# Backward attention loop of an adaLN block: the rows of a head side by side in DRAM, and dQ of two chunks in one PSUM bank

## The chip, the core and the metric

One core of a Trainium2 chip. The time is device microseconds for one execution of the whole program (forward and backward of one block), as the median over runs.

## The reference

The function is one transformer block with conditioning, and the program computes its output and the gradients of nine inputs (x, the attention and MLP weights and biases, the condition c and w_mod). Cut to what matters here:

```python
def _A_ref(x, wqkv, wo):                       # B, S, D = 1, 2048, 512; H = 32; Dh = 16
    q, k, v = ...                              # (x @ wqkv), split by heads
    scores = einsum('bhqd,bhkd->bhqk', q, k) * Dh ** (-0.5)
    p = softmax(scores, axis=-1)
    o = einsum('bhqk,bhkd->bhqd', p, v)
    return o.transpose(0, 2, 1, 3).reshape(B, S, D) @ wo

h = layernorm(x) * (1 + ca) + sa
x = x + ga * _A_ref(h, A_wqkv, A_wo)
h = layernorm(x) * (1 + cb) + sb
x = x + gb * _B_ref(h, B_w1, B_b1, B_w2, B_b2)  # MLP with squared ReLU
_out, _vjp = jax.vjp(_f, A_x, A_wqkv, ...); _grads = _vjp(grad_out)
```

The attention's backward part needs, for each head, E = exp(scores) again, dP = dO V', dS = E * (dP - delta), and from these dV = E' dO, dK = dS' Q and dQ = dS K. A head has only 16 channels and 2048 x 2048 scores, so these products have a short side of 16 and everything is about moving [128 x 512] blocks of scores through the engines.

## The kernel before

The program has four parts: the projections, the forward attention with the MLP and its gradients woven in, the last chunk of the MLP, then the backward attention loop, and the final projections of the gradients. The change is in the backward loop and in what feeds it.

**How the loop is tiled.** Heads go in eight groups of four (`HG`, here called a head for short). Partitions 32h to 32h+15 of a tile hold the 16 channels of head h of the group; partition 32h+16 holds an extra row (the score bound m beside q, minus delta beside dO, ones beside k and v), so one matmul with 32 rows gives scores minus bound, or dP minus delta. A unit is 128 queries by 512 keys for the four heads; four units (512 queries) make a chunk; a head has 4 x 4 chunks (`kc` over keys outside, `qc` over queries inside), the loop 128 chunks.

**What a unit does.** `score` (L1603): for each of four heads one matmul into a PSUM bank, taken in turn from three banks A, B, C. `expo` (L1609): ACT takes the exponential into `E_u`. `dp_pair` (L1623, L1625): two matmuls for a pair of heads into one of two double banks `psD_u`, then DVE multiplies with `E_u` into `dS_u` (four buffers of two units each). `k_quad` (L1663) and `v_quad` (L1672): four matmuls each, for the four heads in column groups of PE, summing dK and dV of 512 keys in the bank `accVK`; ACT moves that out after 16 units (L1675).

**dQ.** It needs dS with keys on the partitions. `transpose_unit` issues DMA transposes on SP's queue, two units in one DMA (L1640) or one (L1638). For every second chunk the last of its four units is turned by PE instead (`pe_turn`, L1653) and copied by ACT (L1769). So of two chunks seven units go by DMA (three doubles, one single) and one by PE. `dq_quad` (L1690) multiplies the turned tile `dsT` (three buffers of a chunk) with the K rows of all 2048 keys, kept in SBUF as `KS_tok`, and sums a chunk in the bank C. Of each group of 32 rows of that bank only 16 hold dQ; the other 16 come from the neighbour's columns and are not used. `dq_out` moves the bank out with ACT (L1700 for the first key block, else L1703), and POOL adds it to `dQacc` (L1708).

**What sets the order.** The order is written out by hand as two strings, one for iterations in which the chunk before is turned on PE (`order_t`, with the tokens t and T) and one for the others (`order_n`). A token names an operation: s and e are score and exponential with their number in the chunk, D a `dp_pair` (with the transposes that it completes, and the DMAs planned for that point), q a `k_quad` or `v_quad`, d half of a `dq_quad` set (two of four key blocks), Q `dq_out`, f a dummy matmul (`keep_warm`). Beside each string stands the list of banks for the sixteen scores. Each engine executes its own instructions in this order; the transposes have SP's queue nearly to themselves. Iterations alternate t, n, t, n. A chunk's dQ is taken two iterations after its scores.

**Loads and stores in the loop.** `plan_head` plans the loads of the next head, issued by ACT (`load`, L1585) at fixed counts of D, one every four: four pieces of q by tokens (`q_st`), four row loads each for k, v, q and dO (16 rows of 4 KB) and one each for m and delta (4 rows of 4 KB), 22 in all. Each block of 512 keys stores dV and dK (128 KB), each head its dQ in four stores of 16 rows of 4 KB, planned at successive counts. `spread_qz` (L1226, POOL) spreads q by tokens. The first head's loads (`head_loads`) and the four loads of `KS_tok` are issued by SP in the last MLP chunk.

**The end.** After the loop SP loads what was stored (L1788, L1789), the weights (L1791), and copies the last head's dQ with four DMAs (L1793), then PE turns all of it (L1944) for the final products.

Of the kernel before, what the change touches and what calls it, by code (L numbers as in the profile page):

```python
# [17 lines left out]
BF = dt.bfloat16  # L18
F32 = dt.float32

P = 128
# [9 lines left out]
QPAD = 528  # L31
# [3 lines left out]
def kernel(  # L35
# [53 lines left out]
    k_st = dram.tile([P, TT, D], BF, name="k_st")  # L89
    v_st = dram.tile([n, D], BF, name="v_st")  # L90
    qkT_st = dram.tile([2, D, n], BF, name="qkT_st")
    vT_st = dram.tile([D, n], BF, name="vT_st")
    dOT_st = dram.tile([D, n], BF, name="dOT_st")
    m_st = dram.tile([H, n], BF, name="m_st")
    d_st = dram.tile([H, n], BF, name="d_st")
# [51 lines left out]
    with ExitStack() as ph:  # L147
# [398 lines left out]
        def fload(qc, hg):  # L546
            i = hg % 2
            kt_sb, qt_sb = kts[i], qts[i]
            rows = list(row_loads(kt_sb, qkT_st[1], hg, slice(0, n)))
            rows += row_loads(qt_sb, qkT_st[0], hg, slice(512 * qc, 512 * qc + 512), m_st)  # L550
            for i, (to, fro) in enumerate(rows):
                later(i // (3 if qc == 0 else 1), sp, to, fro)
            run_due()
            fh[qc, hg] = (qt_sb, kt_sb)
# [203 lines left out]
        qkT_v = qkT_st.rearrange("a (b p) n -> p a b n", p=P)  # L758
# [94 lines left out]
        def prep():  # L853
# [114 lines left out]
            sp(qkT_st[1, 0:P, :], KTs[0][:])  # L968
            sp(qkT_st[0, 0:P, 0:512], sP[:, 4, :])
# [26 lines left out]
        def plan_tasks():  # L996
# [5 lines left out]
            def key_tile(b, g):  # L1002
# [8 lines left out]
                if g == QC - 1:  # L1011
                    later(1, sp, qkT_st[1, b * P:(b + 1) * P, :], KTs[b][:])
# [6 lines left out]
            def query_tile(g, hb):  # L1019
# [7 lines left out]
                if g == 0:  # L1027
                    later(1, sp, qkT_st[0, hb * P:(hb + 1) * P, 0:512], sP[:, lo + hb, :])
                elif hb == 3:
                    later(1, sp, qkT_v[:, 0, :, chunk_cols(g)], sP[:, lo:lo + 4, :])  # L1030
# [38 lines left out]
            def token_tile(which, g, ti):  # L1069
# [9 lines left out]
                if which == 1:  # L1079
                    DVE.tensor_copy(T[key][:, ti, :], pt.rearrange("p b q -> p (b q)"))  # L1080
                    if ti == 3:
                        later(1, sp, k_st[:, gs, :], T[key][:])
                else:
                    tok = T[key].rearrange("p t d -> p (t d)").rearrange("p (g t e) -> p g t e", g=HG, t=4)
                    DVE.tensor_copy(tok[:, :, ti, :], pt.rearrange("p b q -> p (b q)").rearrange("p (g e) -> p g e", g=HG))
                    if ti == 3:
                        later(1, sp, q_st.rearrange("g p t e -> p g t e")[:, :, gs, :], tok)
# [115 lines left out]
        def head_set(i):  # L1203
            strm.append(tc.alloc_tile_pool(name=f"phIs{i}", bufs=1, side="right"))
            hs = {key: strm[i].tile([P, n], BF, name=f"i{key}{i}") for key in ("k", "v", "q", "do")}
# [3 lines left out]
        def head_fill(i):  # L1209
            for key in ("k", "v", "q", "do"):  # L1210
                POOL.memset(hsets[i][key][:], 1.0 if key in ("k", "v") else 0.0)

        def kvq_loads(hg):
            hs = hsets[hg % 2]
            for i in range(4):
                yield hs["qs"][:, 4 * i:4 * i + 4, :], q_st[hg][:, 4 * i:4 * i + 4, :]
            yield from row_loads(hs["k"], qkT_st[1], hg, slice(0, n))
            yield from row_loads(hs["q"], qkT_st[0], hg, slice(0, n), m_st)
            yield from row_loads(hs["v"], vT_st, hg, slice(0, n))

        def spread_qz(hg):
# [3 lines left out]
            else:  # L1225
                POOL.tensor_scalar(to, fro, SCALE, None, ALU.mult)  # L1226

# [14 lines left out]
        def last_chunk(O_c, L, w1T, w2T):  # L1242
# [76 lines left out]
            later(17, copy_const, hsets[0]["v"][:], 1.0)  # L1319
# [50 lines left out]
            keep["KS"] = kpool.tile([P, TT, QPAD], BF, name="KS_tok", tag="ks")  # L1370
            POOL.memset(keep["KS"][:, :, D:QPAD], 0.0)
            for i in range(4):
                later(4 + 3 * i, sp, keep["KS"][:, 4 * i:4 * i + 4, 0:D], k_st[:, 4 * i:4 * i + 4, :])
# [128 lines left out]
        with ExitStack() as ph2:  # L1502
            pools["mm"] = ph2.enter_context(tc.tile_pool(name="psM2", bufs=4, space=bass.MemoryType.PSUM))
            with tc.manual_schedule(engines={PE.engine, ACT.engine, DVE.engine, SP.engine, POOL.engine}):
# [8 lines left out]
                DVE.memset(hsets[0]["q"][:], 0.0)  # L1513
                DVE.memset(hsets[0]["do"][:], 0.0)
                copy_const(hsets[0]["k"][:], 1.0)
# [17 lines left out]
                def head_loads():  # L1533
                    done = slice(0, 512 * (QC - 1))
                    for i, (to, fro) in enumerate(list(kvq_loads(0)) + list(row_loads(hsets[0]["do"][:, done], dOT_st, 0, done, d_st))):
# [9 lines left out]
    KS_tok, dOs_tok = keep["KS"], keep["dOs"]  # L1545
# [11 lines left out]
    with ExitStack() as ph:  # L1557
# [9 lines left out]
        def load_head(hg):  # L1567
            st = dict(hsets[hg % 2])
            st["qz"] = qz[hg % 2]
            st["acc"] = stg.tile([P, n], F32, name="dQacc", tag="dQacc", bufs=1)  # L1570
            st["dq"] = stg.tile([P, n], BF, name="dQst", tag="dQst", bufs=1)
            st["vk"] = stg.tile([P, n], BF, name="vkb", tag="vkb")
            hst[hg] = st


# [11 lines left out]
        def plan_head(hg):  # L1587
            j0 = (hg - 1) * 128 + 14
            loads = list(kvq_loads(hg)) + list(row_loads(hsets[hg % 2]["do"], dOT_st, hg, slice(0, n), d_st))
            for i, (to, fro) in enumerate(loads):  # L1590
                at(j0 + 4 * i, load, to, fro)
            at(j0 + 40, spread_qz, hg)

# [12 lines left out]
        def expo(u, hq):  # L1606
            if hq == 0:
# [37 lines left out]
        def keep_warm():  # L1645
            PE.matmul(cur["vk"][0:DH, :], KS_tok[:, 0, D:QPAD], dOs_tok[:, 0, :], start=False, stop=False,
# [19 lines left out]
        def v_quad(u):  # L1666
# [7 lines left out]
            if qt == TT - 1:  # L1674
# [3 lines left out]
                else:  # L1678
                    part = slice(kc * 512, (kc + 1) * 512)
                    at(cur["j"] + 4, load, dVKtP[hg][:, part], hst[hg]["vk"][:, part])  # L1680

        def dq_quad(b, kt):
            hg, kc, qc, _ = units[4 * b]
            if kt == 0:
                cur["dq"] = psx.tile([P, 512], F32, name="dqacc", tag="px")
            acc = cur["dq"]
            tT = dqt[b]
            for hq in range(4):
                h = hg * 4 + hq
# [370 lines left out]
```

## Time and profile before

| | us |
|---|---|
| median of 3 runs (lowest, highest) | 2517.32 (2511.94, 2524.12) |
| span of the profiled execution | 2517.6 |
| forward part and last MLP chunk | 0 to 1125 |
| backward loop (first exponential to the last) | 1125.3 to 2380.5 |
| final products | 2382 to 2518 |
| busy in the loop, of 1257: PE / ACT / DVE / POOL | 1206 / 1225 / 1186 / 147 |

The profile is of one execution. Its span, first to last instruction, is the only time that it gives of itself; it lies within the runs shown. PE, ACT and DVE are the tensor, scalar and vector engine, POOL is GpSimd, SP the engine that here only issues DMAs; a q behind a name means its queue (waits and DMA issues). A duration in the timeline runs from an instruction's start to its last write; the engine can start the next one before that, so what an instruction costs its engine is the distance between two starts where nothing waits.

### The profile page before, as it was taken

Reading aid. Unit: us, or ns where it says so; the run is one execution under the profiler, and the core shown is the slowest. Engines: PE = TensorE matmul, PEld = TensorE weight load, DVE = VectorE, ACT = ScalarE, POOL = GpSimd, SP = SyncE. Lnnn points to the kernel's source line nnn. Section 1 sums busy time; section 2 is a strip of 40 time slices with the busy share of each in tenths; the row PEclk is TensorE's granted clock in tenths of the full one; section 3 lists DMA queues with packets and bytes.
Section 4 is the critical chain, followed back from the end, with each engine's and each line's share of the span. In section 5 each row is a group of like instructions: output and inputs, shape, how many; then the busy total and the mean of one; then the engine's idle time right before and its main releaser. Section 6 shows DMA issues by size and latency. Waiting matters only on the chain. (4 is left out here: it accounts for less than half of the span.)

```text
span 2517.6 us, 49897 instructions
## 1 busy us (share of the span) xinstructions
PE 2342.5 (93%) x19005; PEld 776.3 (31%) x19005; DVE 1810.1 (72%) x2341; ACT 2302.3 (91%) x3577; POOL 350.0 (14%) x379
## 2 busy tenths in 40 slices
PE   7899889989988999999999999999999999999999
PEld 3232223222322323442233322233323323322343
DVE  5556153454435454579999999999999999998862
ACT  7999999999989999539999999999999999999842
POOL 2000000211323142210111101111010111100100
PEclk9999999999999999999999999999999999998999
DMA  6476455367658766979999999999999999999972
GB/s 202 136 193 165 150 122 139 96 161 144 103 85 176 151 134 119 261 208 191 202 199 210 196 206 208 201 207 202 207 202 202 209 195 203 195 208 212 196 237 72
DMA packets 1220981, 447.15 MB, mean 178 GB/s; under 512 B 1096951, under 2 KB 1191607, under 8 KB 1220486
## 3 DMA queue, kind: packets, MB, share of 16 engines
q1 hardware_dynamic: 1192822, 409.11, 82.2%
q0 software_dynamic: 10944, 16.78, 4.8%
q10 hardware_dynamic: 16976, 18.07, 2.8%
q8 instruction: 149, 2.44, 0.4%
q14 instruction: 90, 0.74, 0.1%
HBM read 96.75 MB, written 73.95 MB: 68 GB/s over the span
## 5 line engine op out<-in xcount | busy, mean ns | idle before, releaser
L1625 DVE TENSOR_TENSOR dS_u<-psD_u,E_u 128x1024 bf16<-128x1024 f32 x1024 | 1186.0, 1218 | 71.6 <-PE psD_u L1623 24.0
L567 ACT ACTIVATE ET<-psST 128x1024 bf16<-128x1024 f32 x1024 | 942.0, 1260 | 27.0 <-PE psST L565 26.5
L1609 ACT ACTIVATE E_u<-psS_A 128x512 bf16<-128x512 f32 x768 | 513.1, 668 | 10.5 <-PE psS_C L1603 8.5
L1609 ACT ACTIVATE E_u<-psS_B 128x512 bf16<-128x512 f32 x768 | 505.8, 659 | 12.1 <-DMA dsT<-dS_u 3.0
L1623 PE MATMUL psD_u<-iv,ido 32*128 32x512 bf16 x2048 | 409.6, 388 | 0.0
L565 PE MATMUL psST<-qt_sb,kt_sb 32*128 32x512 bf16 x2048 | 317.8, 387 | 62.0 <-ACT ET L567 46.6
L1609 ACT ACTIVATE E_u<-psS_C 128x512 bf16<-128x512 f32 x512 | 335.4, 655 | 3.3 <-PE psS_B L1603 1.4
L1603 PE MATMUL psS_B<-ik,iq 32*128 32x512 bf16 x768 | 295.3, 385 | 12.8 <-ACT E_u L1609 5.5
L1603 PE MATMUL psS_A<-ik,iq 32*128 32x512 bf16 x768 | 293.4, 382 | 10.9 <-DVE dwlast L237 1.0
L1603 PEld LDWEIGHTS <-iq 32*128 32x128 bf16 x2048 | 130.2, 91 | 316.1 <-issue 298.8
L1663 PE MATMUL accVK<-dS_u,qz 128*32 128x512 bf16 x2048 | 213.3, 390 | 0.4 <-PE psD_u L1623 0.2
L581 PE MATMUL oacc<-ET,vaug 128*32 128x512 bf16 x2048 | 207.7, 396 | 2.2 <-DVE ostage L585 2.2
L1672 PE MATMUL accVK<-E_u,dOs_tok 128*16 128x512 bf16 x2048 | 204.1, 387 | 0.0
L1708 POOL TENSOR_TENSOR dQacc<-dQacc,dqtmp 128x512 f32<-128x512 f32 x64 | 81.2, 1268 | 852.0 <-ACT dqtmp L1703 852.0
L1603 PE MATMUL psS_C<-ik,iq 32*128 32x512 bf16 x512 | 194.7, 380 | 4.2
L565 PEld LDWEIGHTS <-kt_sb 32*128 32x128 bf16 x2048 | 85.8, 91 | 352.2 <-issue 324.6
L1690 PE MATMUL dqacc<-dsT,KS_tok 128*32 128x512 bf16 x2048 | 146.5, 384 | 18.5 <-DMA dsT<-dS_u 4.3
L1769 ACT ACTIVATE dsT<-ptT 128x1024 bf16<-128x1024 bf16 x128 | 145.8, 1139 | 7.9 <-PE ptT L1653 7.3
L251 DVE COPY part<-pm 128x512 f32<-128x512 f32 (+2 forms) x103 | 63.5, 617 | 114.8 <-PE pm L233 111.5
L1623 PEld LDWEIGHTS <-ido 32*128 32x128 bf16 x2048 | 104.6, 91 | 98.9 <-issue 92.9
L1663 PEld LDWEIGHTS <-qz 128*32 128x32 bf16 x2048 | 58.4, 94 | 177.9 <-issue 162.9
L581 PEld LDWEIGHTS <-vaug 128*32 128x32 bf16 x2048 | 53.1, 93 | 121.4 <-issue 121.4
(407 smaller groups left out, 2516.3 us busy)
## 6 DMA issues: line engine op xcount, KB each, us to landing
p_st<-part POOLq DMA_DIRECT2D x36, 256.0 KB, 5.2
kt_sb<-qkT_st SPq DMA_DIRECT2D x124, 64.0 KB
wA<-in_B_w_dram SPq DMA_DIRECT2D x28, 256.0 KB
wB<-w1T_st SPq DMA_DIRECT2D x21, 256.0 KB
wA<-w2T_st SPq DMA_DIRECT2D x21, 256.0 KB
wB<-in_B_w_dram SPq DMA_DIRECT2D x21, 256.0 KB
p_st<-part POOLq DMA_DIRECT2D x25, 192.0 KB, 5.3
p_st<-part SPq DMA_DIRECT2D x18, 256.0 KB
```

What stands on the lines that cost most here:

```text
L565: PE.matmul(ps[:, hi, :], kt_sb[r:r + 32, kt * P:(kt + 1) * P], qt_sb[r:r + 32, :], start=True, stop=True, tile_position=(r, 0))
L567: ACT.activation(ET[:, 2 * pair:2 * pair + 2, :], ps[:], AF.Exp, scale=SCALE)
L581: PE.matmul(oacc[32 * hq:32 * hq + 32, :], lhsT, ET[:, hq, :], start=(kt == 0), stop=(kt == TT - 1), tile_position=(0, 32 * hq), skip_grou ...
L1603: PE.matmul(psS[:], st["q"][r:r + 32, qt * P:(qt + 1) * P], st["k"][r:r + 32, kc * 512:kc * 512 + 512], start=True, stop=True, tile_positi ...
L1609: ACT.activation(bst[u][0][:, hq, :], sst.pop((u, hq))[:], AF.Exp, scale=SCALE)
L1623: PE.matmul(psD[:, hi, :], st["do"][r:r + 32, qt * P:(qt + 1) * P], st["v"][r:r + 32, kc * 512:kc * 512 + 512], start=True, stop=True, til ...
L1625: DVE.tensor_tensor(dS_u[:, 2 * pair:2 * pair + 2, :], psD[:], E_u[:, 2 * pair:2 * pair + 2, :], ALU.mult)
L1663: PE.matmul(cur["vk"][32 * hq:32 * hq + 32, :], hst[hg]["qz"][:, qt, hq, :], bst[u][1][:, hq, :], start=(qt == 0), stop=False, tile_positi ...
L1672: PE.matmul(acc[32 * hq:32 * hq + DH, :], dOs_tok[:, qt, (hg * 4 + hq) * DH:(hg * 4 + hq + 1) * DH], E_u[:, hq, :], start=False, stop=(qt ...
L1690: PE.matmul(acc[32 * hq:32 * hq + 32, :], KS_tok[:, kc * 4 + kt, h * DH:h * DH + 32], tT[:, :, hq * 4 + kt, :], start=(kt == 0), stop=(kt ...
L1708: POOL.tensor_tensor(dst2, dst, tmp[:], ALU.add)
L1769: ACT.activation(dst, pt[:], AF.Identity)
```

## The change

In the DRAM staging, the transposed rows of k, v, q and dO, before in three tensors, stand side by side per channel (`rows4_st`), and m and delta beside one another (`md_st`). K by tokens is kept by heads, as q was. A head's loads become: K by tokens (one), q by tokens (one), four row loads of 16 rows with k, v, q and dO at once (256 KB each), one for m and delta, planned 13 counts of D apart. dK and dV are stored by pairs of blocks (256 KB).

`KS_tok` goes. In its place two buffers `KZ` hold one head's K each, spread by POOL (`spread_k`) so that 16 zero columns stand on either side of each head's 16. For an even chunk `dq_quad` takes the window whose first 16 columns are K, for an odd one the window whose last 16 are, so that two chunks are summed in the two halves of the 32 rows of one bank. `dq_out` therefore runs once for two chunks, in iterations without turns; an odd chunk's dQ is taken two iterations after its scores as before, an even one's three. `dQacc` and `dQst` have half the columns, and a head's dQ is stored by four DMAs of 32 rows whose destination is ordered x, r, m, c (2 x 16 x 2 x 512).

Both order strings and bank lists are new: every exponential stands right behind its score, scores and exponentials go out of their numbers, five q tokens stand in t and eleven in n, and all four d tokens and the Q stand in n.

```diff
+KW = 2 * DH * 4 + DH
-    k_st = dram.tile([P, TT, D], BF, name="k_st")
-    qkT_st = dram.tile([2, D, n], BF, name="qkT_st")
-    vT_st = dram.tile([D, n], BF, name="vT_st")
-    dOT_st = dram.tile([D, n], BF, name="dOT_st")
-    m_st = dram.tile([H, n], BF, name="m_st")
-    d_st = dram.tile([H, n], BF, name="d_st")
+    k_st = dram.tile([HG, P, TT, 64], BF, name="k_st")
+    rows4_st = dram.tile([D, 4, n], BF, name="rows4_st")
+    kT_st, vT_st, qT_st, dOT_st = (rows4_st[:, i, :] for i in range(4))
+    md_st = dram.tile([H, 2, n], BF, name="md_st")
+    m_st, d_st = (md_st[:, i, :] for i in range(2))
...
-        def kvq_loads(hg):
+        def head_rows(hg, k=4):
             hs = hsets[hg % 2]
-            for i in range(4):
-                yield hs["qs"][:, 4 * i:4 * i + 4, :], q_st[hg][:, 4 * i:4 * i + 4, :]
-            yield from row_loads(hs["k"], qkT_st[1], hg, slice(0, n))
-            yield from row_loads(hs["q"], qkT_st[0], hg, slice(0, n), m_st)
-            yield from row_loads(hs["v"], vT_st, hg, slice(0, n))
+            if hg > 0:
+                yield keep["kst"], k_st[hg]
+            yield hs["qs"], q_st[hg]
+            for h in range(4):
+                i = (hg * 4 + h) * DH
+                yield hs["rows"][32 * h:32 * h + DH, 0:k, :], rows4_st[i:i + DH, 0:k, :]
+            aux = hs["rows"].rearrange("(h c) a n -> c h a n", h=4)[DH]
+            yield aux[:, 2:k, :], md_st[hg * 4:hg * 4 + 4, 0:k - 2, :]
...
+        def spread_k(hg):
+            to = keep["KZ"][hg % 2][:, :, DH:DH + 128].rearrange("p t (h e) -> p t h e", h=4)[:, :, :, 0:DH]
+            POOL.tensor_copy(to, keep["kst"].rearrange("p t (h d) -> p t h d", h=4))
...
+            kz = kpool.tile([P, 2 * TT * KW + TT * 64], BF, name="KZ_tok", tag="ks")
+            POOL.memset(kz[:, 0:2 * TT * KW], 0.0)
...
+        def dq_store(dst, hg, src):
+            for hq in range(4):
+                r = hg % 2 * 64 + hq * DH
+                yield (dst[r:r + DH, :].rearrange("r (m x c) -> x r m c", x=2, c=512),
+                       src[32 * hq:32 * hq + 32, :].rearrange("r (m c) -> r m c", c=512))
...
-            for i, (to, fro) in enumerate(loads):
-                at(j0 + 4 * i, load, to, fro)
+            for i, (to, fro) in enumerate(head_rows(hg)):
+                at(j0 + 13 * i, load, to, fro)
             at(j0 + 40, spread_qz, hg)
+            at(j0 + 44, spread_k, hg)
...
             for hq in range(4):
-                PE.matmul(acc[32 * hq:32 * hq + 32, :], KS_tok[:, kc * 4 + kt, h * DH:h * DH + 32], tT[:, :, hq * 4 + kt, :],
-                          start=(kt == 0), stop=(kt == 3), tile_position=(0, 32 * hq), skip_group_check=True)
+                lo = 32 * hq + DH * (1 - b % 2)
+                PE.matmul(acc[32 * hq:32 * hq + 32, :], KZ[hg % 2][:, kc * 4 + kt, lo:lo + 32], tT[:, :, hq * 4 + kt, :],
+                          start=(k == 0), stop=(k == 7), tile_position=(0, 32 * hq), skip_group_check=True)
...
-            if kc == QC - 1 and qc == QC - 1 and hg < HG - 1:
-                    at(cur["j"] + 6 + hq, load, dQc[hg // 2, r:r + DH, :], st["dq"][32 * hq:32 * hq + DH, :])
+            if kc == QC - 1 and qc == QC - 2 and hg < HG - 1:
+                for i, (to, fro) in enumerate(dq_store(dQc[hg // 2], hg, st["dq"])):
+                    at(cur["j"] + 6 + 4 * i, load, to, fro)
...
         order_t = (
-            "s0 s1 q s2 e0 e1 D s3 D e2 s4 e3 t1 e4 q T1 D "
-            "s5 s6 e5 f f t2 e6 s7 T2 e7 D s8 e8 D f f s9 e9 q q s10 "
-            "s11 e10 D d1 d2 e11 Q q s12 D e12 s13 e13 q s14 D e14 "
-            "s15 q q e15 ").split(), "ABCABBABACABABCA"
+            "s0 e0 s2 e2 f s1 e1 D s3 e3 D s6 e6 s4 e4 t1 T1 q s5 e5 D q s11 e11 s7 e7 D q q s9 "
+            "e9 s8 e8 D t2 T2 D s10 e10 f f D s13 e13 s12 e12 q D s15 e15 s14 e14 f ").split(), "CBACBAACBAABCBBA"
         order_n = (
-            "s0 D s1 q e0 q s2 e1 e2 D s3 s4 q s5 e3 D e4 "
-            "e5 s6 q s7 D s8 e6 e7 d1 e8 s9 D d2 e9 q Q s10 "
-            "s11 e10 D q s12 e11 e12 s13 e13 D q s14 s15 e14 e15 D q ").split(), "CBACBACBABABCABC"
+            "q s1 e1 D s0 e0 q q s2 e2 D s3 e3 q q s4 e4 D s5 e5 d1 d3 s6 D s7 e7 e6 d2 d4 Q "
+            "q D s8 e8 s13 q e13 s9 e9 D s10 e10 q s11 e11 D s12 e12 q q s15 e15 s14 e14 q D ").split(), "ACBCABBAACABCBBA"
...
+                    elif c == "d" and 0 <= b - 3 < NU // 4:
+                        for kt in (2 * ((i - 1) % 2), 2 * ((i - 1) % 2) + 1):
+                            dq_quad(b - 3 + (i - 1) // 2, kt)
```

At the end of the loop the last head's dQ is copied by eight DMAs (`dq_rows`, 16 rows of two pieces) in place of four. Elsewhere the program only follows the new names and layouts.

## The prediction

> **What bounds the kernel now.** I read the page first, then the windows over the backward loop, then its timeline, then the waits.
>
> The windows show the loop (first exponential at 1125.3 us, last ending at 2380.5) with no engine idle:
>
> ```profile
> core 0: us, PE busy (x) PEld busy (x) DVE busy (x) ACT busy (x) POOL busy (x), PEclk, DMA share, GB/s
> 1245.00:1400.00 155.00, 149.30 (x1446) 47.10 (x1445) 148.51 (x129) 153.49 (x294) 17.95 (x13) 1.00 1.21 202
> ```
>
> Busy share does not rank engines here, because durations overlap on ACT and DVE. The timeline gives the real spacing (start us, duration us, engine, line):
>
> ```profile
> 1701.26 15.98 SPq L1640 DMA_TRANSPOSE dsT<-dS_u  x3
> 1701.33 11.40 DVE L1625 TENSOR_TENSOR dS_u<-psD_u,E_u 128x1024 bf16<-128x1024 f32 x10 [0.37 <-PE psS_B L1603]
> 1702.20 0.62 ACT L1609 ACTIVATE E_u<-psS_C 128x512 bf16<-128x512 f32 x1
> 1702.67 0.63 ACT L1609 ACTIVATE E_u<-psS_A 128x512 bf16<-128x512 f32 x1
> ...
> 1703.19 0.40 PE L1663 MATMUL accVK<-dS_u,qz 128*32 128x512 bf16 x4
> 1703.42 0.39 PE L1672 MATMUL accVK<-E_u,dOs_tok 128*16 128x512 bf16 x4
> 1703.74 0.38 PE L1603 MATMUL psS_A<-ik,iq 32*128 32x512 bf16 x1
> ...
> 1708.46 0.60 ACT L1703 ACTIVATE dqtmp<-dqacc 128x512 f32<-128x512 f32 x1
> 1708.95 0.59 ACT L1609 ACTIVATE E_u<-psS_A 128x512 bf16<-128x512 f32 x1
> ...
> 1714.19 1.17 ACT L1769 ACTIVATE dsT<-ptT 128x1024 bf16<-128x1024 bf16 x1
> 1715.10 0.75 ACT L1609 ACTIVATE E_u<-psS_B 128x512 bf16<-128x512 f32 x1
> ```
>
> To be seen: an exponential holds ACT 0.477 us (1702.20 to 1702.67), a dQ eviction 0.49 (1708.46 to 1708.95), a copy of turned tiles 0.91 (1714.19 to 1715.10). Ten DVE multiplies last 11.40, so one comes every 1.131. On PE a column quad (four matmuls side by side) follows another after 0.22, but a quad and then a score are 0.32 apart: 0.10 for the change between row and column tiling. A double DMA transpose holds SP's queue about 5.3 us.
>
> Now the ledger of a pair of iterations (one with turns, t, and one without, n), two chunks. The starts of L1609 give t 10.79 and n 8.53 (medians). Of 63 pairs 47 last 19.26 in the mean; the other 16 are longer by 22.8 us together.
> - ACT: 32 x 0.477 = 15.26, turned copies 1.82, two dQ evictions 0.98, the accVK eviction every second pair 0.24: 18.30. It stands 19.26 - 18.30 = 0.96.
> - DVE: 16 x 1.131 = 18.10.
> - SP's queue, summed over its transposes: 1193 us, 18.6 a pair. Its fastest doubles take 4.8, its singles 1.7: 16.1 at best.
> - PE shows 149.3 of 155 busy, but the ends of its matmuls are modelled; a count of its work in n stands under the slower rival.
>
> So ACT sets the pace, DVE is 0.2 behind, and the transposes follow.
>
> **The change part by part.**
>
> dQ of two chunks in one bank. The even chunk's K columns write rows 0 to 15 of each group of 32 and the odd chunk's rows 16 to 31, the other half adding zeros. The dQ matmuls stay 16 a chunk; evictions fall from 128 to 64, POOL adds from 96 to 48 (L1708, 1.27 us each, POOL idle 86%: worth nothing). ACT saves 0.49 a pair: 17.81 is left, now below DVE's 18.10.
>
> The new orders. I walked a steady pair by hand with the durations above, 0.65 from an exponential's start to its bank being free, 0.39 from a score's start to its exponential. In t the banks go round C, A, B without a break, the two turns taking C's place, and ACT waits at no token: 16 x 0.477 + 1.82 = 9.45. In n three places hold it. s6 takes bank B right after s5, so it waits for e5, and s7 stands behind s6 on PE: ACT stands 0.62 before e7. s4 follows two column quads and comes 0.18 late. The end of n costs about 0.15. Together 0.95 against 0.96 before, so the pair is 17.81 + 0.95 = 18.76, or 0.50 less; 64 pairs: -32 us. What covers the burst: its two halves (four quads, 0.86 each) run while ACT does e4, e5 and then e7, e6, and between DVE's D3 and D5 PE is away 1.3 us against 1.13 a multiply, which the two psD banks absorb. If that cover goes, each D5 comes up to 0.4 late, 26 us in all.
>
> What waits behind the burst: PE works in order, so d3 needs the odd chunk's last transpose. Before, d1 stood after e7; now d3 stands after e5, and 9.7 us of slack (supply of the single to its use, less its transfer) become 7.8. In the trace the single starts 2.2 to 9.7 us after its data are ready, 7.7 or more in 9 of 64 pairs. The even chunk is read a whole iteration later and gains slack.
>
> Loads: 22 a head become 7, of up to 256 KB, plus K (256 KB a head, before 2 MB in four loads ahead of the loop). Bytes per head rise from 2.1 to 2.3 MB, against 29 MB of transposes. An ACT issue of 0.31 between two exponentials left them 0.477 apart, so fewer issues save nothing by count. But the five rows of L1585 for the first dQ store, 1.06 to 1.30 us each, delay the next exponential by about 0.6, and at 1464 us ACT stood 3.0 until a transpose landed. The stores now come four multiplies apart: -6 us (0 to -12).
>
> The dQ stores have a destination whose outer dimension is 2. In the trace's DMA packets a load of 16 rows leaves sixteen 4-byte completion packets, one per engine, a load of 4 rows (m, d) four. So I expect the store on two engines: 4 stores x 32 packets of 1 KB x 0.046 us (median of such packets here) = 5.9 us on each, before 4 x 0.159 = 0.6. Transposes use all engines and wait for the slowest: +5.3 a head, +37 us in seven heads if nothing hides it, 0 if the slack does. The lag in the first two pairs of a head is mostly 3.5 to 6, so 2 to 4 of the 7.8 are left to hide it: about 1.1 a head gets through, +8 us. No row has an outer dimension of 2, so this is read on from 16 and 4. The Trainium skill ("DMA: Bandwidth & Descriptors", Rules for kernel authors) speaks against this edit outright: an outermost dimension below 16 confines a DMA to at most that many engines. With none of it hidden the sum would be 2518.
>
> spread_k adds one POOL copy a head, nearest row L1226 at 2.8 us, POOL being idle: nothing. The memset of KZ (4608 columns; L1211 takes 1.8 for 2048, so about 4) lies in a stage where POOL waits 45.8 us. SP issues some 15 DMAs fewer before the loop: 0 to -3, I take 0. At the end the last dQ goes in 8 pieces, not 4 (L1793 takes 0.76 apiece): 0 to +3, mostly behind 3.8 MB of loads; +1. In the forward part only K's token store changes shape: nothing.
>
> Sum against the profiled execution (span 2517.6; the times list no other figure for it, and the median of the runs is 2517.3, so nothing worth a term lies around): 2517.6 - 32 - 6 + 8 + 1 = 2488.6. Half a per cent, 12.6 us, is about what a measurement of this kernel tells from no change.
>
> **The rivals.**
>
> *The stands go as well.* If e5 is early enough that s6 never waits, DVE bounds the pair at 18.10 plus 0.2: 2517.6 - 64 x 0.96 = 2456. For it: DVE's spacing does not move off 1.131 for long stretches. Against: bank B is used twice running, and the transposes need 16.1 to 18.6. The Trainium skill (same page, Latency and other measured facts) gives 261 GB/s for a DMA transpose with a broken middle dimension; an estimate by it is 14.1 us for a pair's 3.67 MB, and the transposes would then never bind. The fastest rows here, 16.1, say otherwise. Chance 0.15.
>
> *The saving does not arrive.* PE stands at d3 for late transposes, or D5 comes late, and the stands grow by the 0.5 that the eviction freed: 2517.6 - 6 + 8 + 1 = 2521. For it: nine lags already at 7.7 or more. Chance 0.15.
>
> *Slower: PE becomes the bound of n.* n gets 11 + 8 = 19 column quads for 8 + 4 = 12. If the n of before hides none of it, n is 8.53 + 7 x 0.215 = 10.04, while t falls only to ACT's 9.45 + 0.24 and its old stand of 0.6, 10.29: a pair of 20.33, +68 us, with the other terms 2589. It decides once PE's idle time in an n is under about 1.1 us (n over 8.97). Against it: 12 quads at 0.215, 16 changes of tiling at 0.10 and 11 rounds of scores make 6.6 of 8.53, leaving 1.9. For it: the profile shows PE 96% busy. Chance 0.17.
>
> **How the numbers follow.** The forecast has 0.50, at 2489 with 2465 to 2510 as its own range; 0.03 is for what I do not see. Faster by over 0.5%: most of 0.50, all of 0.15, a little of the third: 0.64. Within: 0.15. Slower: 0.21. The range reaches down to the DVE-bound case and up into the PE-bound one: 2448 to 2552.
>
> **What would show it.** Right: 64 dQ evictions on ACT; L1609's starts giving a t near 9.5 to 9.8 and an n near 9.1; ACT standing before e7 in every n; dQc stores with two completion packets. Wrong: an n above 9.8 with PE unbroken (the slower rival); pairs still at 19.2 with PE waiting on DMA dsT; SP's sum above 1230 us; pairs at 18.3 with DVE unbroken. If t stays above 10.2, my walk of t is wrong.

## The result, and the profile after

| | before | after |
|---|---|---|
| median of all runs, us | 2517.8 | 2583.5 |
| ratio after to before, 95% interval | | 1.0247 [1.0209, 1.0285] |
| span of the profiled execution, us | 2517.6 | 2569.8 |
| first exponential of the loop, us | 1125.3 | 1130.4 |
| last exponential ends, us | 2380.5 | 2431.4 |
| SP's queue, summed over the transposes, us | 1193 | 1240 |
| clock at half within the loop: stretches, us | 8, 44 | 23, 147 |

The change made the program 2.5% slower. The profiled execution is the quickest of the four after and shows 52 us of the 66, 46 of them inside the loop. Seen through the same window as before (busy us and counts, then granted clock and DMA):

```profile
core 0: us, PE busy (x) PEld busy (x) DVE busy (x) ACT busy (x) POOL busy (x), PEclk, DMA share, GB/s
1245.00:1400.00 155.00, 144.60 (x1368) 42.07 (x1366) 139.79 (x121) 140.10 (x268) 10.87 (x8) 0.94 1.14 190
```

ACT, which had 153.5 of 155 us, now has 140.1; DVE and PE fell too. No engine took ACT's place: all three stand. The clock was granted at 0.94 where it had been 1.00.

**The undisturbed pair came as forecast, but saved less.** 31 of 63 pairs last 18.98 us in the mean; the corresponding 44 of before last 19.26. The burst in n, from the timeline (start, duration):

```profile
1414.72 0.60 ACT L1628 ACTIVATE E_u<-psS_A 128x512 bf16<-128x512 f32 x1
1414.89 1.05 PE L1710 MATMUL dqacc<-dsT,KZ_tok 128*32 128x512 bf16 x16
1415.22 0.59 ACT L1628 ACTIVATE E_u<-psS_B 128x512 bf16<-128x512 f32 x1
...
1415.88 0.38 PE L1622 MATMUL psS_A<-irows 32*128 32x512 bf16 x1
1416.19 1.05 PE L1710 MATMUL dqacc<-dsT,KZ_tok 128*32 128x512 bf16 x16
1416.34 0.60 ACT L1628 ACTIVATE E_u<-psS_A 128x512 bf16<-128x512 f32 x1 [0.53 <-PE psS_A L1622]
```

e5 starts at 1415.22, e7 at 1416.34: 1.12 later, of which 0.48 is e5 and about 0.65 standing for s7, which comes behind d1, d3 and s6.

**The other 32 pairs are 86 us longer together** (before, 19 pairs and 23 us). Three groups make nearly all of it. First, late transposes. The waits from 1140 us to the end of the loop (us in total, times, longest), after and then, for dqacc, before:

```profile
ACT E_u L1628 <- PE psS_A L1622: 76.2, 74, 7.5
...
PE dqacc L1710 <- DMA dsT<-dS_u: 31.9, 15, 6.1
...
DVE dS_u L1644 <- DMA dsT<-dS_u: 13.3, 9, 3.9
```

```profile
PE dqacc L1690 <- DMA dsT<-dS_u: 1.6, 1, 1.6
```

One of them in the timeline:

```profile
1375.83 0.74 PE L1710 MATMUL dqacc<-dsT,KZ_tok 128*32 128x512 bf16 x8 [2.91 <-DMA dsT<-dS_u]
...
1376.51 0.60 PE L1622 MATMUL psS_A<-irows 32*128 32x512 bf16 x1
...
1377.19 0.60 ACT L1628 ACTIVATE E_u<-psS_A 128x512 bf16<-128x512 f32 x1 [4.12 <-PE psS_A L1622]
```

PE stands at d3 for the odd chunk's last transpose, s6 and s7 stand behind d3, and ACT, 4.12 us, behind s7. ACT's stands at e7 and e8 beyond those of an undisturbed pair sum to 49 us, nearly all of it in 15 of the n. The cause is on SP's queue, beside the loads of the next head. Its transposes after, and then before, at the same place (three doubles, one single, and so on):

```profile
1182.09 18.21 SPq L1659 DMA_TRANSPOSE dsT<-dS_u  x3
1200.35 3.87 SPq L1657 DMA_TRANSPOSE dsT<-dS_u  x1
1204.39 15.62 SPq L1659 DMA_TRANSPOSE dsT<-dS_u  x3
1220.11 5.51 SPq L1657 DMA_TRANSPOSE dsT<-dS_u  x1
```

```profile
1174.61 16.62 SPq L1640 DMA_TRANSPOSE dsT<-dS_u  x3
1191.33 2.46 SPq L1638 DMA_TRANSPOSE dsT<-dS_u  x1
1193.95 16.08 SPq L1640 DMA_TRANSPOSE dsT<-dS_u  x3
1210.15 3.38 SPq L1638 DMA_TRANSPOSE dsT<-dS_u  x1
```

A pair's four transposes take 22.1 and 21.1 us where they took 19.1 and 19.5. Over the eight pairs of a head the mean is 20.2, 20.7, 21.2, 20.0, 19.5, 18.2, 17.6, 17.7 after, and 18.9, 18.9, 19.2, 18.8, 19.1, 18.7, 18.0, 17.6 before. Before, every one of these is below the pair's 19.26; after, the first five are above the pair's 18.98, so the lag grows from pair to pair until PE stands. A least-squares fit of each transpose's excess on the DMAs beside it gives the 28 row loads of 256 KB 58 us (the row loads of before about 25) and the dQ stores 37 (before 9). These shares are estimates: a fit on the time of the packets gives 54 and 28.

Second, the clock. Two iterations t in which nothing waits for a transpose, one at full clock, one in which half the clock was granted for 6.8 us:

```profile
1402.70:1412.50 9.80, 9.14 (x80) 3.20 (x78) 9.72 (x10) 9.80 (x19) 0.00 (x0) 1.00 1.37 202
1421.90:1432.50 10.60, 10.16 (x70) 3.26 (x69) 8.88 (x9) 9.62 (x18) 0.00 (x0) 0.68 1.12 199
```

Twelve pairs have such a t and take 20.7 us or more, 20 us together; before there were five of some 1.4. Twelve of the 23 stretches begin between the fourth and the sixth exponential of t, behind the seam of n and t; nine begin in n, most of them where PE stands at d3. All starts are multiples of 3.413 us apart, and all but the first last 3.41 or 6.83. Third, about 7 us in the first pair (before 4) and some 10 where stores are issued on ACT (before 12 to 13).

The ledger, profile to profile: undisturbed pairs 62 x -0.28 = -17, late transposes +49, clock +13, first pair +3, store issues -3: 45 of the 46 us in the loop; the loop starts 5 us later and the end takes 1 more.

### The profile page after: what moved, and what is told of

The parts are those of the page before. It is cut to its first block, busy times and chain, and to the rows that moved or that the text cites. A ratio compares the mean times of both kernels' runs of the same rounds, so it can differ in the third digit from the quotient of the medians.

```text
span 2569.8 us, 49511 instructions
## 1 busy us (share of the span) xinstructions
PE 2364.3 (92%) x19002; PEld 761.4 (30%) x19002; DVE 1810.1 (70%) x2341; ACT 2266.6 (88%) x3513; POOL 300.6 (12%) x339
## 4 chain that ended last, share of the span: by engine, by line
PE 44%; ACT 27%; DVE 11%; DMA 9%; issue 7%; SPq 1%; POOL 0%; ACTq 0%; DVEq 0%; POOLq 0%
ACT E_u L1628 15%; ACT ET L566 9%; DMA dsT<-dS_u 6%; PE psST L564 4%; DVE dS_u L1644 4%; PE dqacc L1710 3%; PE accVK L1682 3%; PE psD_u L1642 3%; PE pm L232 3%; PE ptT L1672 3%; PE accVK L1691 2%; PE oacc L580 2%; PE psS_B L1622 2%; PE psS_A L1622 2%; PE pdh L1902 2%
## 5 line engine op out<-in xcount | busy, mean ns | idle before, releaser
L1628 ACT ACTIVATE E_u<-psS_A 128x512 bf16<-128x512 f32 x768 | 498.3, 649 | 90.4 <-PE psS_A L1622 77.8
L1642 PE MATMUL psD_u<-irows 32*128 32x512 bf16 x2048 | 439.7, 398 | 25.6 <-DVE dS_u L1644 19.4
L1622 PE MATMUL psS_A<-irows 32*128 32x512 bf16 x768 | 305.8, 398 | 2.5 <-ACT E_u L1628 1.2
L1622 PE MATMUL psS_B<-irows 32*128 32x512 bf16 x768 | 302.0, 393 | 1.8 <-ACT E_u L1628 0.9
L1691 PE MATMUL accVK<-E_u,dOs_tok 128*16 128x512 bf16 x2048 | 222.6, 398 | 0.0
L1622 PE MATMUL psS_C<-irows 32*128 32x512 bf16 x512 | 197.9, 386 | 6.1 <-ACT dsT L1787 4.8
L1622 PEld LDWEIGHTS <-irows 32*128 32x128 bf16 x2048 | 122.4, 91 | 255.9 <-issue 255.9
L1710 PE MATMUL dqacc<-dsT,KZ_tok 128*32 128x512 bf16 x2048 | 147.8, 406 | 37.0 <-DMA dsT<-dS_u 36.3
L1642 PEld LDWEIGHTS <-irows 32*128 32x128 bf16 x2048 | 124.0, 91 | 190.2 <-issue 173.3
L1730 POOL TENSOR_TENSOR dQacc<-dQacc,dqtmp 128x512 f32<-128x512 f32 x32 | 40.5, 1267 | 767.2 <-ACT dqtmp L1725 749.2
L1672 PE MATMUL ptT<-identb,dS_u 128*128 128x128 bf16 x1024 | 87.4, 235 | 12.8 <-DVE dS_u L1644 0.7
```

Of the source, the lines that this page charges most:

```text
L1622: PE.matmul(psS[:], st["q"][r:r + 32, qt * P:(qt + 1) * P], st["k"][r:r + 32, kc * 512:kc * 512 + 512], start=True, stop=True, tile_positi ...
L1628: ACT.activation(bst[u][0][:, hq, :], sst.pop((u, hq))[:], AF.Exp, scale=SCALE)
L1642: PE.matmul(psD[:, hi, :], st["do"][r:r + 32, qt * P:(qt + 1) * P], st["v"][r:r + 32, kc * 512:kc * 512 + 512], start=True, stop=True, til ...
L1672: PE.transpose(pt[:, i, :], held["dS"][:, 2 * half + i // 4, kt * P:(kt + 1) * P], identb[:])
L1691: PE.matmul(acc[32 * hq:32 * hq + DH, :], dOs_tok[:, qt, (hg * 4 + hq) * DH:(hg * 4 + hq + 1) * DH], E_u[:, hq, :], start=False, stop=(qt ...
L1710: PE.matmul(acc[32 * hq:32 * hq + 32, :], KZ[hg % 2][:, kc * 4 + kt, lo:lo + 32], tT[:, :, hq * 4 + kt, :], start=(k == 0), stop=(k == 7), ...
```

## The experiments

Each was timed in five rounds against the kernel before, whose medians were 2516.3 to 2517.9 us there; "after" is 2583 us throughout. Waits, sums and stretches are those of one profiled execution of each kernel.

**e1 and e2: the two costs on the queue, one at a time.**

```
e1: for to, fro in dq_rows(...): at(cur["j"] + 6 + 2 * i, load, to, fro)      # was dq_store, 4 * i
e2: for a in range(k): yield hs["rows"][32*h:32*h+DH, a, :], rows4_st[i:i+DH, a, :]   # was 0:k
    at(j0 + 4 * i, load, to, fro)                                                # was 13 * i
```

> The changed kernel with one edit: the dQ rows of a head are stored by eight DMAs whose outer dimension is 16 (one per head and half), two multiplies apart, where the change has four with an outer dimension of 2. Measured on the changed kernel: SP's queue sums 1240 us over its transposes (before: 1193); a least-squares fit of each transpose's excess on the DMAs beside it gives the dQ stores 36 us of that (before 9) and the loads of the four rows 58 (before about 25); ACT stands about 46 us at e7 beyond its standing in undisturbed pairs. Theory 'store on two engines': the sum falls to about 1213, the dQ share to about 9, and about 15 us of the 46 go, the ones in the first pairs of a head: 2568 by the median of 2583. Rival 'the row loads make the stands': the sum falls the same, but the stands stay above 40 and the time above 2578. Rival 'the store is not confined': the sum stays at 1240.

> The changed kernel with one edit: from the second head on, the loads of 256 KB (four rows of 16 channels, 16 KB in one packet on each DMA engine) are split by tensor into four loads of 64 KB with packets of 4 KB, issued four multiplies apart instead of thirteen. Theory 'large packets': the share of the row loads in the transposes' excess falls from 58 us to about 25, SP's sum from 1240 to about 1207, and the stands at e7 from 46 to 25 or so: 2563. Rival 'bytes, not packets': the loads cost the transposes the same 58 us in smaller pieces, the sum stays at 1240, the time within 5 us of 2583. Rival 'the dQ stores make the stands': the sum falls to 1207 but the time stays above 2575.

e1: 2555.0, ratio 1.0144 [1.0116, 1.0171]; SP's sum 1210, the dQ stores' share 11. e2, which leaves the first head's loads as they are: 2556.1, ratio 1.0147 [1.0126, 1.0167]; sum 1222, the row loads' share 19. The wait, in e1 and then in e2:

```profile
PE dqacc L1710 <- DMA dsT<-dS_u: 10.2, 5, 3.9
```

```profile
PE dqacc L1714 <- DMA dsT<-dS_u: 17.9, 11, 3.6
```

Both theories hold, and both gave more time than forecast (28 and 27 us against 15 and 20), though e2's sum stayed above the 1207 forecast. Why they gave more is not shown.

**e6: the row loads alone, in the kernel before.** Its orders, its dQ and its K stay; the rows of a head come by four DMAs of 256 KB.

> The kernel before, its orders and its dQ untouched, with one part of the change alone: k, v, q and dO rows of a head side by side in DRAM and loaded by four DMAs of 256 KB (and one for the m and d rows), thirteen multiplies apart. Theory 'large packets slow the transposes and only slack hides it': SP's sum rises from 1193 by about 30; the old order has d1 behind e7 and two multiplies more slack, so under half of it comes through: 2517 + 5 to 15. Rival 'the slowed transposes cost whatever the order': 2517 + 25 or more. Rival 'the load shape is harmless and e2 worked by its spacing': SP's sum stays within 8 us of 1193, the time within 4 us of 2517.

2549.2, ratio 1.0139 [1.0105, 1.0173]; SP's sum 1221, the row loads' share 53. The old order hides none of it: +32 us, the rival's answer.

```profile
PE dqacc L1700 <- DMA dsT<-dS_u: 11.4, 8, 3.2
DVE dS_u L1635 <- DMA dsT<-dS_u: 7.3, 5, 2.9
```

This is the change's loading by itself, and it costs half of what the change cost. With 19 us of transposes in a pair of 19.26 there was no rate to spare, whatever the slack of a single transpose. e2 and e6 change the distance between loads together with their size, so they do not separate the two; for the size speaks that the transposes which meet a large load are the long ones (the last section has one).

**e3: more slack for the odd chunk.** `d1 d3 ... d2 d4` became `d1 d2 ... d3 d4`.

> The changed kernel with one edit in the order of n: the two halves of the even chunk (d1 d2) go where d1 d3 stood, the two of the odd chunk (d3 d4) where d2 d4 stood, behind e7 and e6. The odd chunk's last transpose is needed about 1.6 us later; the work is the same. Theory 'slack': the transposes stay as slow (SP's sum 1240) but the stands at e7 fall from 46 us to about 25, 2562. Theory 'whatever the transposes do, PE is the bound': the sum of e7's stands stays and the time is within 5 us of 2583. Rival 'SP's queue itself is the bound where loads run': the stands only move to another token, time above 2575.

2591.7, ratio 1.0298 [1.0256, 1.0339]. ACT's standing before e7 (0.66 a pair, 40 us, is that of undisturbed pairs) fell from 79 to 47 us, but before e8 it rose from 14 to 40, SP's sum stayed (1244), and dqacc still waited 28.6. The second rival is right: where the queue is too slow for the pair, a later use only moves the stand.

**e12: the queue relieved instead of the loads.** The single transpose of the odd chunk is left out and its place filled with zeros, so part of dQ is missing.

```
if qi == 2: POOL.memset(dqt[u // 4][:, qi], 0.0)      # was the single DMA transpose
```

> The changed kernel, loads and stores as the change has them, but the single transpose of the odd chunk is left out and its place in dsT filled by GpSimd with zeros (so part of dQ is missing). SP's sum falls by 64 x 2.2 to about 1100, 17.2 us a pair. Theory 'the queue's rate': in the first five pairs of a head the transposes of the changed kernel need 19.5 to 21.2 us a pair where an undisturbed pair takes 18.98, so the lag grows until PE stands at d3; with 17.5 to 19 they fit, the waits of dqacc for dsT fall from 32 us to under 6 and the extra stands at e7 from 49 us to under 10: 2583 - 40 = 2543, what is left being the clock. Rival 'single late transposes, not the rate': waits of dqacc for dsT stay above 15 us, time above 2560.

2520.6, ratio 1.0016 [0.9993, 1.0038]: 63 us less than after, with the loads and stores as the change has them. SP's sum is 1044 (the single's place is free for the doubles) and no wait of dqacc for dsT is left. The edit gives the queue more room and also takes away the transpose that lands last, so e12 alone does not tell rate from lateness; e3 does, where more slack at the same rate only moved the stand. What remains of e12's long pairs is the first and 17 of 20.7 to 20.9 us with the clock at half, mostly about 116 us or one pair apart:

```profile
1371.50:1392.20 20.70, 20.26 (x181) 5.76 (x180) 18.60 (x17) 19.14 (x37) 3.02 (x2) 0.84 1.00 179
1392.20:1413.10 20.90, 20.46 (x181) 5.93 (x180) 18.67 (x17) 18.80 (x36) 3.01 (x2) 0.84 1.00 175
1413.10:1432.10 19.00, 18.33 (x181) 5.45 (x180) 18.33 (x17) 18.48 (x37) 3.01 (x2) 1.00 1.00 155
```

Nearly the same instruction counts, 1.7 to 1.9 us more at 0.84: the clock costs time by itself, with no transpose late.

**e4: filling matmuls at the seam of n and t.** Five more `f`: behind e15 and at the end of n, behind e0 and two D at the start of t.

> The changed kernel with five more filling matmuls (f) a pair: one behind e15 and one at the end of n, one behind e0 and two behind multiplies at the start of t. Measured on the changed kernel: the clock is granted at half in 23 stretches of 3.4 to 13.7 us within the loop, 133 us in all (before 44 us), nearly all starting at the fourth exponential of t; 11 of 63 pairs last 20.71 to 20.77, 1.55 more than an undisturbed one, and are those pairs. Theory 'clock': fewer than 6 such stretches besides the first, no pairs of 20.7, 15 to 20 us less: 2566. Rival 'PE has no room there': t of an undisturbed pair grows from 9.67 by 0.2 or more, 64 x 0.2 = 13 us, and eats the gain: 2580. Rival 'the clock follows the standing, not the seam': the stretches stay.

2607.6, ratio 1.0368 [1.0337, 1.0399]. The stretches fell from 23 to 9, none of them at that place in t, but undisturbed pairs grew from 18.98 to about 20.4: each `f` shows as some 0.15 us of standing on the next exponential, the one at the end of n as 0.80. The clock follows what PE does at the seam, and PE has no room there.

**e5, e10: both loads mended.** e5 is e1 and e2 together; e10 also starts the head loads 20 multiplies later (`at(j0 + 20 + 4 * i, ...)`).

> The changed kernel with the edits of e1 and e2 together: dQ stores with an outer dimension of 16, row loads of 64 KB with 4-KB packets. e1 took 28 us off the changed kernel's 2583 and e2 27. Theory 'two separate costs of the transposes': they add up, 2528, SP's sum 1190 to 1195 as before the change, and no long waits of dqacc for dsT left (under 5 us in all, 32 in the changed kernel). Rival 'they share one stall': removing either lets most of the other hide, so both give 2540 or more. What is left above 2500 is then the half-clock stretches (about 20 in e1 and e2, 8 before) and the smaller saving of an undisturbed pair (19.26 to 18.98, 18 us, not 32).

> The kernel of e5 with its head loads begun 20 multiplies later, behind the eight dQ stores of the head before instead of among them (both are issued on ACT). In e5 no wait of dqacc for dsT was left and SP's sum was 1187, below the 1193 before the change, yet it took 2553: in the second and third pair of each head, where stores and loads are issued together, ACT stood 1.0 to 2.8 us before e13 and 1.2 to 3.4 before the next e0, about 24 us in all. Theory 'crowded ACT queue': those stands go, 2553 - 20 to 24 = 2530. Rival 'the stores alone': the stands stay, within 6 us of 2553.

e5: 2552.7, ratio 1.0148 [1.0123, 1.0173], no better than either alone, though SP's sum is 1187 and dqacc waits for no transpose. Neither theory foresaw why: stores and loads are now issued together on ACT, and ACT stands before e13 and before the e0 of t, about 24 us. Two issues before such a stand, the one at its end, and the e0 behind it:

```profile
1329.68 0.56 ACTq L1608 DMA_DIRECT2D dQc<-dQst  x1
...
1330.72 1.03 ACTq L1608 DMA_DIRECT2D irows<-rows_st  x1
...
1335.99 0.57 ACTq L1608 DMA_DIRECT2D dQc<-dQst  x1
1336.67 0.60 ACT L1632 ACTIVATE E_u<-psS_C 128x512 bf16<-128x512 f32 x1 [3.30 <-DMA dsT<-dS_u]
```

ACT stands until the store at 1335.99 is issued. The profile puts the end of the stand down to a transpose; what the issue waits for no run shows.

e10: 2532.0, ratio 1.0064 [1.0044, 1.0085]: with the loads moved away from the stores those stands are gone and the 20 us with them. The two costs of the queue then make 51 us together, close to 28 and 27.

**e11, e16: the clock without more work.** `f` behind e2 and the first `q` of t change places; in e11 on top of e10, in e16 in the changed kernel.

```
"s0 e0 s2 e2 q s1 e1 D s3 e3 D s6 e6 s4 e4 t1 T1 f s5 e5 ..."      # was "... e2 f ... T1 q ..."
```

> The kernel of e10 with the filling matmul after e2 and the first quad of t (behind T1) having changed places: no work is added, a quad of four matmuls over 128 rows comes into the stretch in which the half-clock stretches begin, and a single filling matmul goes out of it. Theory 'the clock follows what TensorE does in that stretch': half-clock stretches fall from about 20 to 10 or fewer, the pairs of 20.7 us (12 of 63 in e5, 1.6 to 1.75 above an undisturbed one) go with them, 12 to 20 us less than e10. Rival 'the clock follows the standing of PE elsewhere': stretches and time stay as in e10, within 5 us. Rival 'the quad comes too early': PE waits for DVE there, t grows by 0.3 or more, slower than e10.

> The changed kernel with only the exchange of e11 (the filling matmul behind e2 and the first quad of t change places); loads and stores as the change has them. Theory 'clock and queue are separate costs': half-clock stretches fall from 23 to about 10 (those that follow a stand of PE at d3 stay), 13 to 18 us less than the changed kernel: 2567. Rival 'shorter t pairs only make the transposes later': the stretches fall but the stands at e7 grow by as much, time within 5 us of 2583.

e11: 2516.3, ratio 0.9994 [0.9979, 1.0008], 16 us below e10; stretches 16 to 5, pairs of 20.5 to 20.85 from 13 to 2. The mean granted clock was 0.957 to 0.972 in e10's nine runs and 0.979 to 0.987 in e11's twelve. The granted clock over 40 slices, after and then e11:

```profile
PEclk9999999999999999989999898999998999999999
```

```profile
PEclk9999999999999999998999999999999999999999
```

e16: 2574.4, ratio 1.0211 [1.0175, 1.0247]; its interval overlaps that of the changed kernel, so the 9 us are not shown. The stretches fell only from 23 to 18, not to about 10 as forecast, but one of them begins at the seam where twelve did; the others are mostly in n, where PE stands. The pairs of 20.5 to 20.85 fell from 9 to 2, the granted clock rose to 0.970 to 0.979 (0.949 to 0.961 in the changed kernel), but in the profile SP's sum rose to 1272 and this wait from 31.9:

```profile
PE dqacc L1710 <- DMA dsT<-dS_u: 55.0, 18, 8.9
```

This fits the rival: shorter t leave the transposes still less time, so the two costs hide each other in part.

**e8, e9: other places for the dQ quads, on e5.** e8 takes the old orders and puts d1 to d4 singly into n; e9 keeps the new ones and spreads the burst (`d1 s7 D e7 s6 d3 e6 d2 s8 D e8 d4 Q`).

> The kernel of e5 with the orders of the kernel before, save for the dQ tokens: those of t are gone, and n has d1, d2, d3, d4 each between two exponentials behind e7 instead of two bursts. One eviction a pair is saved as in the change. Theory 'the new orders cost what the eviction saves, by PE and by the clock': pairs of 18.8 or less, half-clock stretches back to about 8, 2517 - 25 to 30 = 2490. Rival 'PE is the bound of n': with 16 dQ quads' work in n, n grows from 8.54 by more than t loses (10.79 to 10.3): pairs of 19.2 or more, 2515 or above.

> The kernel of e5 with one stretch of n reordered: d1 to d4 stand singly, each behind another exponential (d1 s7 e7 s6 d3 e6 d2 s8 e8 d4 Q), where e5 has two bursts of two. In the changed kernel ACT stands 0.66 us before e7 in an undisturbed pair. Theory 'the burst makes the stand': the 0.66 falls to 0.2 or less, n from 9.02 to about 8.6, 25 us below e5. Rival 'PE has no room in n whatever the order': the stands of n keep their sum of about 1.0 and only change their tokens; the time is within 8 us of e5's.

e8: 2614.2, ratio 1.0372 [1.0329, 1.0415]: n 10.11, t 10.50 (medians), undisturbed pairs 20.2. The numbers are those of the prediction's third rival (n 10.04, t 10.29, pair 20.33), but not by its count: e8's n has 16 quads, the changed kernel's 19. So the count alone does not give n; where the quads stand matters. e9: 2568.2, ratio 1.0196 [1.0173, 1.0220]: n grows from 9.02 to 9.68; the stand at e7 falls to 0.16 but e8 and e13 take 0.74 and 0.46. In both, PE is what ACT waits for, here in e9:

```profile
ACT E_u L1632 <- PE psD_u L1646: 53.2, 84, 1.2
```

Quads in a burst cost less here than quads spread out. The spreading adds four changes of tiling to n, at the prediction's 0.10 an estimated 0.4 of the 0.66; the rest is not accounted for. With the old orders, as e8 has them, the eviction's saving does not show at all.

**e13, e14, e15: what is left.** e13 issues the dQ stores on GpSimd (on e11); e14 splits head 0's row loads too (on e11); e15 adds e3's order to e14.

> The kernel of e11 with the dQ stores issued by GpSimd's queue instead of ACT's. Theory 'an issue on ACT costs an exponential its time': the stores' rows on ACT (0.56 to 0.79 us each, 56 of them) go and ACT's stands in the first pairs of a head with them, 5 to 15 us below e11. Rival 'GpSimd's packets slow the transposes more': SP's sum rises by 10 or more and the time is at or above e11's.

> The kernel of e11 with head 0's row loads, ahead of the loop, split by tensor as well (48 to 64 KB instead of 192 KB). Theory 'large loads on SP's queue delay dwbuf': the 3 us between 1031 and 1090 go, 2516 - 3 = 2513. Rival 'the memset of KZ': the loop still begins 3 us late, 2516.

> The kernel of e14 with d1 d2 in the first place and d3 d4 in the second (the edit of e3). In e11 the waits of dqacc for dsT sum to 14 to 17 us and the extra stands at e7 to about 23. Theory 'slack pays once the queue fits on average': they fall by half, 8 to 12 us below e14: 2503, faster than the kernel before by 0.5%. Rival 'the stands only move to e8, as in e3': within 4 us of e14.

e13: 2520.7, ratio 1.0007 [0.9991, 1.0024], no gain; SP's sum is 1210 against e11's 1207, so the rival's cost does not show in it either. e14: 2514.1, ratio 0.9985 [0.9970, 1.0000]: its loop starts at 1126.1 us and e15's at 1124.3, where the 13 other profiles with the changed loads of head 0 have 1126.9 to 1134.7 (before 1125.3). KZ's memset is still there, so this speaks for the 192-KB loads on SP's queue as the cause; the 2 us of the median are within the noise. e15: 2515.1, ratio 0.9984 [0.9968, 1.0000]: dqacc's wait halves (13.4 to 6.4) and the time does not move. The mended versions are level with the kernel before; none is shown faster.

## Why the prediction was wrong

The forecast was 2489 us, with 2448 to 2552 as its range, and the measured time is 2583.5, 95 us later. The row loads make some 30 of these, the dQ stores 20 more than the 8 reckoned, the saving 15 less than forecast, the clock 13 to 16. These come from different runs, the stands overlap, and the rest is not divided.

- **The eviction and the walk of the orders: right in mechanism, half in size.** There are 64 dQ evictions. t has 9.67 or, with the accVK eviction, 10.15 (forecast 9.45 and 0.24 in the mean), n 9.02 to 9.12 (9.1), ACT stands 0.66 before e7 in every n (0.62). ACT's stands sum to 1.17 a pair instead of 0.95. Those of n sum to 0.94, as forecast; the 0.22 more are in t, where I had counted none, some 0.15 of it before e9. The saving is 0.28 a pair, -17 us, not -32.
- **The step that failed: the loads, costed at nothing.** "An ACT issue of 0.31 between two exponentials left them 0.477 apart, so fewer issues save nothing by count", and the bytes rise only from 2.1 to 2.3 MB. Both are true and neither is the cost. A row of 16 KB is one packet: 1.43 us (median) against 0.159 for one of 4 KB, so a load of the same rows holds all 16 DMA engines more than twice as long. On SP's queue that was +33 us by the fit, and e6 shows +32 us of time for this loading alone. The Trainium skill ("DMA: Bandwidth & Descriptors", Rules for kernel authors) advises to coalesce many small transfers into one large one; beside this stream of transposes the runs show the opposite, and the measurement decides.
- **The dQ stores: price nearly right, cover wrong.** Each store leaves two 4-byte packets, and by the fit the stores' share on the queue rose by 28 us against the 37 reckoned with nothing hidden. The Trainium skill's rule ("DMA: Bandwidth & Descriptors", Rules for kernel authors) that an outermost dimension below 16 confines a DMA to at most that many engines is borne out. But "about 1.1 a head gets through, +8 us" was wrong: e1 took 28 us off. I weighed slack, the lag of a single transpose against its use, where the rate decides: 18.6 us of transposes a pair in the mean, 19 beside loads, against a pair that was to shrink to 18.76. The row was in my own ledger.
- **The saving does not arrive.** That rival named the place, PE at d3 for late transposes, and its sign, "nine lags already at 7.7 or more". It let the stands grow by 0.5 in every pair and put no price on slower loads; they grew by 49 us, nearly all in 15 of the 63 n, and these are the stands that the loads and the stores bring about.
- **PE as the bound of n.** Not in the changed kernel: its n is 9.1. e8 and e4 show how near it is.
- **Not seen at all: the clock.** I read 1.00 in one window and 0.98 over the loop and asked no more. The new t begins with scores and multiplies and few quads, and the clock falls to half there in 12 stretches instead of 5, in the loop in 23 instead of 8. With the loads mended that was worth 16 us (e10 to e11).
- **The rest.** Tail +1, as forecast. The issues ahead of the loop, taken at 0 with 0 to -3, go with a loop that starts 5 us later, by their size as far as e14 shows. The store issues on ACT saved roughly 3 of the 6. KZ's memset took 3.94 (about 4) and cost nothing that e14 shows.
- **The signs.** "SP's sum above 1230" was named as one that would prove me wrong; it is 1240. The 64 dQ evictions, ACT's stand before e7 and the two completion packets came as the signs of being right.

## What to carry to other kernels

Compare the rate of a queue with the period that the change aims at, stage by stage and at the worst place of a head, before asking how much slack a single transfer has: a queue that needs 19 us of 19.26 is a bound already, though it never shows in the waits. When loads share DMA engines with a stream that must keep time, the packet (one contiguous row) is the size that counted here, not the number of issues or the bytes; price such a load by itself, as e6 does. And when an order is rewritten, look at what TensorE does in every stretch of a few us, not only whether it is busy.

## What the hardware showed that was not expected

- Sixteen packets of 16 KB, one to a DMA engine, take 1.43 us each beside transposes; the same bytes in 4-KB packets 4 x 0.159 = 0.64. The double transpose that met the load at 1188.5 us took 8.29 us; half of the doubles take 4.9 to 5.6.
- The clock fell to half at the seam after a step of 3.41 us in which the profile has PE 90 to 94% busy, but (in the changed kernel's profile) with only 17 to 22 matmuls begun, mostly of 32 rows, against 27 to 36 in the step before it. Other steps with 19 matmuls and 94% kept the full clock, so neither figure decides alone. One quad in place of one filling matmul there stopped most of it: the eight profiles with the new t have 8 to 15 such stretches at the seam, the five with the exchange 0 to 2. Starts and lengths lie on a grid of 3.413 us that the loop's own period runs through: every 34 steps, 116 us, the seam meets it again, so the number of stretches differs from run to run. The Trainium skill ("TensorE: Matmul & The Clock Gate", Part 1: The HAM clock gate) has this free-running window of 3413 ns, and the trace agrees; it ties the fall to an idle window, and what counts as idle here no run has separated.
- ACT stands for up to 3.4 us where loads and stores follow each other on its queue within a few us (e5), though the issues' own rows are 0.3 to 1.0; across a lone issue of 0.31 to 0.56 the exponentials stay 0.48 to 0.49 apart in the median.
